# Half and whole slots share first products and transposes; VectorE adds the halves (two MoE layers behind a sparse attention)

## The chip, the cores and the metric

One Trainium2 chip, one of its cores. The metric is the device time of the program in microseconds; a run's time is that of one execution, and the profile is of one execution with its own time. PE is the engine of the matrix products (PEld its weight loads), DVE is VectorE, ACT is ScalarE, POOL is GpSimd, SP issues most transfers.

## What is computed

Attention over 2304 tokens of width 512 (local windows and global tokens), and then twice a layer of experts: every token picks one of 8 experts, and the layer is two products with that expert's weights.

```python
def _moe_ref(x, expert_emb, tau, w1, w2):
    ...
    expert_idx = np.argmax(logits, axis=1)
    ...
    for e in range(8):
        mask = expert_idx == e
        h = np.maximum(x[mask] @ w1[e], 0.0)      # 512 -> 1024
        out[mask] = gate_w[mask, None] * (h @ w2[e])   # 1024 -> 512
def reference(**kwargs):
    ...
    x = _moe_ref(x=x, **moe_kwargs)
    return _moe2_ref(x=x, **moe2_kwargs)   # the same, with a second gate
```

## The kernel before, in words

After the attention each layer sorts its tokens by expert into slots of 128 rows. There are 21 slots in the main path of a layer (three more are code that runs only with over 21 slots in use), and which expert a slot belongs to is known only when the kernel runs. So the code is one stretch per slot, written out for all slots, and branches inside it pick what a slot needs by a mode that PE, ACT and DVE read into registers (`look_mode`, L794; `flag`, L774):

- M_HALF (0): at most 64 tokens, which happens in the last slot of an expert;
- M_FOLLOW (1) and M_LEAD (3): two neighbouring slots of one expert that are multiplied together, all of it in the lead's stretch, while the follower runs two tiny placeholder products (`little`);
- M_SOLO (2): a whole slot by itself. Slot 0 of a layer has no mode and runs as a whole slot.

Products are made of float32 numbers split in two parts, high and low: high by high, high by low and low by high are summed in PSUM. A whole slot needs 24 products of 128x512 for the first layer of weights (`mm1`, L927), then 8 transposes of the result (`hsplit`, L991), ReLU and split into high (ACT) and low (DVE), and 24 products for the second (`mm2`, L1044). A half slot puts the high parts of its 64 tokens in columns 0 to 63 of one operand and their low parts in columns 64 to 127. Then 8 products with the high weights and 8 with the low weights (the latter with the 64 high columns alone, L940 with `m=HALF`) do, and `hsplit` adds the two halves while it turns them: 8 products of float32 by the matrix `twice`, 128x64, two identities over each other (L999). In `mm2` a half slot has 16 products (`half_products`, L986); what its rows 64 to 127 gathered is added on DVE (L1081).

The order of one step s on PE is: `mm1(s)`, in layer 0 the routing work of earlier slots (transposes L1098, products L233 and L240, L1167 and L1168), `mm2(s-1)` in two stretches of four weight blocks with the transposes of slot s+2 between them (L850, `xsplit`), `hsplit(s)`. In the same step ACT copies and DVE subtracts the next expert's weights into high and low parts (`split1`, `split2`, L757 to L767: 1024 columns per instruction), if the next slot belongs to another expert. The order is written by hand; the queues run in order on each engine, and semaphores join them.

`any_of` (L818) and `either` (L798) write the branches. Where one arm of a branch is empty, the engine that skips the other arm runs an instruction that waits for its own earlier work and then adds to its semaphore what the skipped arm would have added. Before the change both arms of PE's branches in the slots hold products.

Of the kernel before, what the change touches and what calls it, by code (L numbers as in the profile page):

```python
# [9 lines left out]
F32 = mybir.dt.float32  # L10
# [4 lines left out]
AF = mybir.ActivationFunctionType  # L15
ALU = mybir.AluOpType
AX = mybir.AxisListType
# [3 lines left out]
P = 128  # L21
# [10 lines left out]
HALF = P // 2  # L32
# [3 lines left out]
M_HALF, M_FOLLOW, M_SOLO, M_LEAD = range(4)  # L36
# [4 lines left out]
XR = 3  # L41
# [64 lines left out]
def sparse_attention_two_moe(ctx, tc, qt, kt, vx, vn, qg, emb, tau, w1a, w2a, wgo, w1b, w2b, cs1, cs2, out):  # L106
    nc = tc.nc
    V, S, G, T, SP = nc.vector, nc.scalar, nc.gpsimd, nc.tensor, nc.sync
# [25 lines left out]
    twice = cp.tile([P, HALF], F32, name="twice")  # L134
# [526 lines left out]
    class Slots:  # L661
# [265 lines left out]
        def mm1(self, s, amid=None):  # L927
            self.room(s)
            if self.leads(s):
                self.room(s + 1)  # L930
            ph = [ps_h.tile([P, 512], F32, name="ph") for n in range(2)]
            self.ph[s] = [ps_ht.tile([P, 512], F32, name="pht") for n in range(2)]
            self.h[s] = [mp.tile([P, 512], F32, name=f"hs{n}", bufs=1) for n in range(2)]
            ws = [[(w1h[k][:, n * 512:(n + 1) * 512], w1l[k][:, n * 512:(n + 1) * 512]) for n in range(2)]
                  for k in range(4)]

            def some(x, part, first, last, m=P):
                for k in range(4):
                    for n in range(2):
                        T.matmul(ph[n][:m], lhsT=x[:, k, s % XR, :m], rhs=ws[k][n][part], start=first and k == 0,  # L940
                                 stop=last and k == 3, skip_group_check=True)

            def half():

                some(xh, 0, True, False)
                some(xh, 1, False, True, HALF)

            def whole():
                some(xh, 0, True, False)
                some(xh, 1, False, False)  # L950
                some(xl, 0, False, True)

            def full(ks):
                for k in ks:
                    for n in range(2):
                        self.full_products(ph[n], xh[:, k, s % XR], xl[:, k, s % XR], *ws[k][n], k == 0, k == 3)

            def little():

                for p in ph:  # L960
                    T.matmul(p[:, 0:1], lhsT=onesb, rhs=ones[:, 0:1], start=True, stop=True)

            if amid:
                for a, z in zip([0] + sorted(amid), sorted(amid) + [4]):
                    if a:
                        amid[a]()
                    full(range(a, z))
            else:
                arms = {T: (half, little, whole, lambda: self.lead_products(s, ph, 0))}

            def keep():
                for n in range(2):
                    S.copy(self.h[s][n], ph[n])  # L973

            if amid:
                keep()
            else:
                self.any_of(s, {**arms, S: (keep, None, keep, None)})
            return ph

        def full_products(self, out, ah, al, bh, bl, first, last):
            T.matmul(out, lhsT=ah, rhs=bh, start=first, stop=False, skip_group_check=True)
            T.matmul(out, lhsT=ah, rhs=bl, start=False, stop=False, skip_group_check=True)
            T.matmul(out, lhsT=al, rhs=bh, start=False, stop=last, skip_group_check=True)

        def half_products(self, out, a, bh, bl, first, last):  # L986

            T.matmul(out, lhsT=a, rhs=bh, start=first, stop=last, skip_group_check=True)
            T.matmul(out[:HALF], lhsT=a[:, :HALF], rhs=bl, start=False, stop=last, skip_group_check=True)

        def hsplit(self, s, later=None):  # L991
            hs, pos = self.h.pop(s), self.ph.pop(s)
            pts = [p.rearrange("p (k t) -> p k t", k=4) for p in pos]
            his, los = self.room(s)

            def half():
                for pt, h in zip(pts, hs):
                    for k in range(4):
                        T.matmul(pt[:, k, :HALF], lhsT=h[:, k * P:(k + 1) * P], rhs=twice, start=True, stop=True)  # L999

            def full():
                for pt, h in zip(pts, hs):
                    for k in range(4):
                        T.transpose(pt[:, k, :], h[:, k * P:(k + 1) * P], ident)

            def half_low():
                for pt, hi in zip(pts, his):
                    V.scalar_tensor_tensor(out=hi[:, :, HALF:], in0=pt[:, :, :HALF], scalar=0.0,
                                           in1=hi[:, :, :HALF].bitcast(F32), op0=ALU.max, op1=ALU.subtract)

            def full_low():
                for pt, hi, lo in zip(pts, his, los):
                    V.scalar_tensor_tensor(out=lo, in0=pt, scalar=0.0, in1=hi.bitcast(F32),
                                           op0=ALU.max, op1=ALU.subtract)

            def little():
                for p in pos:
                    T.matmul(p[:, 0:1], lhsT=onesb, rhs=ones[:, 0:1], start=True, stop=True)

            single = [lambda: [S.activation(hi[:, :, :HALF], pt[:, :, :HALF], AF.Relu) for pt, hi in zip(pts, his)],  # L1020
                      lambda: [S.activation(hi, pt, AF.Relu) for pt, hi in zip(pts, his)]]
            arms = {T: (half, little, full, lambda: self.lead_products(s, pos, 1)), S: (single[0], None, single[1], None)}
            if later is None:
                arms[V] = (half_low, None, full_low, None)
            self.any_of(s, arms)
            if later is not None:
                later += [lambda pt=pt, hi=hi, lo=lo: V.scalar_tensor_tensor(
                    out=lo, in0=pt, scalar=0.0, in1=hi.bitcast(F32), op0=ALU.max, op1=ALU.subtract)
                    for pt, hi, lo in zip(pts, his, los)]
            return pos  # L1030
# [13 lines left out]
        def mm2(self, s, amid=None, after=None, last=False):  # L1044
            his, los = self.hT.pop(s)
            hT = [(hi[:, k, :], lo[:, k, :]) for hi, lo in zip(his, los) for k in range(4)]
            py = (ps_h.tile([P, DM], F32, name="pye", tag="ph") if s + self.l == 0 else
                  ps_ht.tile([P, DM], F32, name="pyl", tag="pht") if last else ps_y.tile([P, DM], F32, name="py"))
            amid = amid or {}

            def ws(k):
                return w2h[k // 2][:, k % 2], w2l[k // 2][:, k % 2], k == 0, k == 7

            def whole(ks):

                for x, w in ((0, w2h), (1, w2h), (0, w2l)):
                    for k in ks:
                        T.matmul(py, lhsT=hT[k][x], rhs=w[k // 2][:, k % 2], start=k == 0 and x == 0 and w is w2h,  # L1058
                                 stop=k == 7 and w is w2l, skip_group_check=True)

            if s + self.l == 0:
                self.mm2_early(py, hT)
            for a, z in zip([0] + sorted(amid), sorted(amid) + [8]) if s + self.l else ():
                if a:
                    amid[a]()
                self.either(s, {T: (lambda: [self.half_products(py, hT[k][0], *ws(k)) for k in range(a, z)],
                                    lambda: whole(range(a, z)))})
            if after:
                after()
            yr = (mp.tile([P, DM], F32, name="yr", bufs=3) if s or self.l else  # L1070
                  sm.tile([P, DM], F32, name="yr0", tag="sq1", bufs=1))
            gate = self.gt.pop(s)[:, 0:1]
            S.activation(yr, py, AF.Copy, scale=gate)  # L1073
            self.y[s] = yr

            if (s, V.engine) not in self.mode:
                return
            yl = mp.tile([P, DM], F32, name="yl", tag="yT")[:HALF]

            def half():  # L1080
                V.scalar_tensor_tensor(out=yr[:HALF], in0=yl, scalar=gate[:HALF], in1=yr[:HALF],  # L1081
                                       op0=ALU.mult, op1=ALU.add)

            self.either(s, {S: (lambda: S.copy(yl, py[HALF:]), None), V: (half, None)})
# [289 lines left out]
    first = First(0)  # L1374
# [13 lines left out]
    xh, xl = [wx.tile([P, 4, XR, P], F32R, name=f"x{w}") for w in "hl"]  # L1388
# [9 lines left out]
    for v in range(3):  # L1398
        m = c[:, C_MASK + v * P:C_MASK + (v + 1) * P].rearrange("p (a t) -> p a t", a=4)
# [406 lines left out]
    def rest():  # L1806
        yield from norms
        yield from r4.gating()
        yield from [None] * 4
        yield from r4.storing(S)  # L1810
        yield from r3.storing()
# [81 lines left out]
```

## Time and profile before

| what | us |
|---|---|
| runs of the kernel before | 733.7, 737.54, 743.43 (median 737.54) |
| the profiled execution, its own time | 737.24 |
| its span, first to last instruction | 735.5 |
| PE busy | 648.6 (88%) |
| DVE busy | 422.3 (57%) |
| ACT busy | 361.4 (49%) |

The attention takes the span to about 172 us, layer 0's slots run from there to about 470 us, layer 1's from about 480 us to the end. An execution's own time is 1.7 us more than its span. A view of lines groups instructions by source line; a timeline merges neighbours of one line and gives the idle time of the engine ahead of them in brackets, with what ended it. "issue" as the cause is an engine that waited for nothing that the profile shows; a name with q is the engine's sequencer, which runs branches and semaphore instructions.

### The profile page before, as it was taken

To read this page: it belongs to the slowest core of one execution; us is meant where nothing else is said; L and a number is where in the kernel's file an instruction comes from. 1 tells how busy PE (TensorE), PEld (TensorE's weight loads), DVE (VectorE), ACT (ScalarE), POOL (GpSimd) and SP (SyncE) were. 2 spreads that over 40 slices of the span, in tenths; PEclk is the share of its full clock that TensorE was granted. 3 is DMA by queue.
4 is the path that set the end of the run, shared out by engine and by line. 5 is a ranking of instruction groups with operands and counts; after the bars stand their busy time and mean duration, and the time that the engine had idled before them with its cause. 6 is when DMAs were issued, how large, how long until landed. Compare 5 with 4: busy or idle time off the path is not lost. (4 is left out here: it accounts for less than half of the span.)

```text
span 735.5 us, 20018 instructions
## 1 busy us (share of the span) xinstructions
PE 648.6 (88%) x6289; PEld 522.6 (71%) x6297; DVE 422.3 (57%) x1210; ACT 361.4 (49%) x881; POOL 214.9 (29%) x291
## 2 busy tenths in 40 slices
PE   7877776877999899898898989798999999999994
PEld 3555454556878798787676867577797889788893
DVE  4657878895226845467467877741474444364340
ACT  3667766821234633455355744411574444473540
POOL 3453636104412211131120500041243324245131
PEclk9999999988999899999999999899999999999998
DMA  9984949303437514548567425233756444736500
GB/s 277 265 288 143 304 118 259 86 23 75 143 108 217 161 46 143 173 137 234 165 168 211 124 90 204 85 91 133 271 184 243 150 163 156 239 107 205 179 27 27
DMA packets 55156, 118.05 MB, mean 161 GB/s; under 512 B 13800, under 2 KB 15336, under 8 KB 54961
## 3 DMA queue, kind: packets, MB, share of 16 engines
q1 hardware_dynamic: 44544, 87.21, 38.4%
q0 software_dynamic: 9344, 27.91, 12.3%
q8 instruction: 98, 1.61, 1.0%
q14 instruction: 98, 0.79, 0.5%
q10 hardware_dynamic: 1072, 0.53, 0.3%
HBM read 100.11 MB, written 16.30 MB: 158 GB/s over the span
## 5 line engine op out<-in xcount | busy, mean ns | idle before, releaser
L643 DVE TENSOR_TENSOR kq<-st,kq 128x1024 fp32r<-128x1024 f32 x64 | 75.4, 1220 | 70.7 <-ACT kq L765 62.8
L643 DVE TENSOR_TENSOR w2l<-st,w2h 128x1024 fp32r<-128x1024 f32 x64 | 74.4, 1219 | 13.1 <-ACT w2h L765 9.5
L1089 POOL DMA_INDIRECT out<-yr,ti x21 | 34.1, 1622 | 149.8 <-ACTq L757 71.3
L680 POOL DMA_INDIRECT xrow<-xs,idx x40 | 51.0, 1274 | 91.3 <-DVE all L592 37.7
L1058 PE MATMUL py<-w2h,hh 128*128 128x512 f32 x240 | 71.7, 421 | 3.2 <-issue 3.1
L940 PE MATMUL ph<-kq,xh 128*128 128x512 f32 (+1 forms) x256 | 64.4, 404 | 5.8 <-DVEq L757 1.3
L1058 PE MATMUL py<-w2l,hh 128*128 128x512 f32 x240 | 66.4, 399 | 0.7 <-issue 0.7
L1058 PE MATMUL py<-w2h,hl 128*128 128x512 f32 x240 | 66.4, 399 | 0.0
L1073 ACT ACTIVATE yr<-py,gt 128x512 f32<-128x512 f32 x39 | 26.8, 688 | 68.5 <-PE py L1058 43.6
L765 ACT CAST kq<-st 128x1024 fp32r<-128x1024 f32 x56 | 55.9, 1048 | 4.3 <-ACTq L740 2.8
L940 PEld LDWEIGHTS ph<-kq,xh 128*128 128x128 f32 (+1 forms) x256 | 43.5, 175 | 20.4 <-issue 2.8
L892 PE MATMUL ph<-xh,kq 128*128 128x256 f32 x384 | 53.8, 302 | 4.8 <-DVE xl L854 2.2
L765 ACT CAST w2h<-st 128x1024 fp32r<-128x1024 f32 x56 | 54.5, 1047 | 5.7 <-ACTq L827 3.4
L696 POOL TENSOR_SCALAR va<-gt 128x1 f32<-128x1 f32 x21 | 4.6, 220 | 174.6 <-DVE oh L1123 174.2
L892 PEld LDWEIGHTS ph<-xh,kq 128*128 128x128 f32 x384 | 51.3, 208 | 5.2 <-ACTq L757 1.6
L1058 PEld LDWEIGHTS py<-w2l,hh 128*128 128x128 f32 x240 | 46.2, 192 | 11.5 <-issue 1.1
L1058 PEld LDWEIGHTS py<-w2h,hl 128*128 128x128 f32 x240 | 46.2, 193 | 10.8
L892 PE MATMUL pht<-xh,kq 128*128 128x256 f32 x384 | 49.6, 285 | 4.1 <-ACTq L757 2.1
L680 POOL DMA_INDIRECT gt<-gs,idx x40 | 47.8, 1194 | 17.4 <-issue 8.6
L892 PEld LDWEIGHTS pht<-xh,kq 128*128 128x128 f32 x384 | 47.2, 191 | 7.0 <-ACTq L757 3.0
L1058 PEld LDWEIGHTS py<-w2h,hh 128*128 128x128 f32 x240 | 42.4, 194 | 9.8 <-issue 3.3
L973 ACT COPY hs<-ph 128x512 f32<-128x512 f32 x34 | 18.4, 589 | 61.5 <-PE ph L940 59.1
(540 smaller groups left out, 1348.4 us busy)
## 6 DMA issues: line engine op xcount, KB each, us to landing
st<-in_w1a SPq DMA_DIRECT2D x32, 512.0 KB, 6.8
st<-in_w2a SPq DMA_DIRECT2D x32, 512.0 KB, 5.1
st<-in_w1b SPq DMA_DIRECT2D x32, 512.0 KB, 6.7
st<-in_w2b SPq DMA_DIRECT2D x32, 512.0 KB, 7.0
xs<-yr SPq DMA_DIRECT2D x21, 256.0 KB, 7.7
kq<-in_kt POOLq DMA_DIRECT2D x3, 1728.0 KB, 9.3
xs<-xrow SPq DMA_DIRECT2D x17, 256.0 KB, 4.2
vw<-in_vx SPq DMA_DIRECT2D x26, 128.0 KB, 7.6
```

Of the source, the lines that this page charges most:

```text
L643: V.tensor_sub(lo[k], st[k], hi[k].bitcast(F32))
L680: G.indirect_dma_start(out=to, out_offset=None, in_=rows_[self.l][:n, :], in_offset=bass.IndirectOffsetOnAxis(ap=idx, axis=0), bounds_chec ...
L696: G.tensor_scalar(out=self.va[s], in0=tok, scalar1=FAR, scalar2=None, op0=ALU.is_lt)
L765: S.copy(hi[k], st[k])
L892: T.matmul(po, lhsT=w[k][:, f * P:(f + 1) * P], rhs=x[:, k, at], start=first and k == 0 and f % 2 == 0, stop=last and k == 3, skip_group_c ...
L940: T.matmul(ph[n][:m], lhsT=x[:, k, s % XR, :m], rhs=ws[k][n][part], start=first and k == 0, stop=last and k == 3, skip_group_check=True)
L973: S.copy(self.h[s][n], ph[n])
L1058: T.matmul(py, lhsT=hT[k][x], rhs=w[k // 2][:, k % 2], start=k == 0 and x == 0 and w is w2h, stop=k == 7 and w is w2l, skip_group_check=True)
L1073: S.activation(yr, py, AF.Copy, scale=gate)
L1089: G.indirect_dma_start(out=out, out_offset=bass.IndirectOffsetOnAxis(ap=self.ti.pop(s), axis=0), in_=yr, in_offset=None, bounds_check=NTOK ...
```

## The change

`half` and `whole` of `mm1`, of `hsplit` and of `mm2` become one stretch each that both run, and what only whole slots need stands behind a branch without an Else:

- `mm1`: the 8 products with the high weights and the 8 with the low weights, now all with 128 columns of the left operand, are shared (`shared`); the 8 with the low part of x (`rest`) stand behind `m > M_HALF`. The order of the tests is another: lead first, then follow, then the shared stretch.
- `hsplit`: half slots run the 8 transposes of whole slots. DVE then sums the two halves of a half slot out of PSUM into two new tiles `hsum`, in a branch of its own in front of the one for the split, and ACT and DVE read these tiles in place of PSUM.
- `mm2`: in each stretch high by high, then high by low run for all; low by high stands behind `m > M_HALF`. Half slots use all 128 columns for the low weights too.

```diff
+            def shared():
                 some(xh, 0, True, False)
-                some(xh, 1, False, True, HALF)
-            def whole():
-                some(xh, 0, True, False)
-                some(xh, 1, False, False)
+                some(xh, 1, False, True)
+            def rest():
                 some(xl, 0, False, True)
...
-                arms = {T: (half, little, whole, lambda: self.lead_products(s, ph, 0))}
+                self.first_products(s, shared, rest, little, lambda: self.lead_products(s, ph, 0))
...
+        def first_products(self, s, shared, rest, little, lead):
+            m = self.mode.get((s, T.engine))
+            if m is None:
+                shared()
+                if rest:
+                    rest()
+                return
+            def single():
+                with tc.If(m == M_FOLLOW) as follows:
+                    little()
+                with follows.Else():
+                    shared()
+                    if rest:
+                        with tc.If(m > M_HALF):
+                            rest()
+            if self.leads(s):
+                with tc.If(m > M_SOLO) as both:
+                    lead()
+                with both.Else():
+                    single()
+            else:
+                single()
...
-            def half():
-                for pt, h in zip(pts, hs):
-                    for k in range(4):
-                        T.matmul(pt[:, k, :HALF], lhsT=h[:, k * P:(k + 1) * P], rhs=twice, start=True, stop=True)
...
-            arms = {T: (half, little, full, lambda: self.lead_products(s, pos, 1)), S: (single[0], None, single[1], None)}
+            self.first_products(s, full, None, little, lambda: self.lead_products(s, pos, 1))
+            arms = {S: (single[0], None, single[1], None)}
+            if (s, V.engine) in self.mode:
+                sums = [mp.tile([P, 4, HALF], F32, name="hsum", bufs=2) for _ in pts]
+                with tc.If(self.mode[s, V.engine] < M_FOLLOW):
+                    for a, pt in zip(sums, pts):
+                        V.tensor_reduce(a, pt.rearrange("p k (h t) -> p k t h", h=2), axis=AX.X, op=ALU.add)
...
-                self.either(s, {T: (lambda: [self.half_products(py, hT[k][0], *ws(k)) for k in range(a, z)],
-                                    lambda: whole(range(a, z)))})
+                some(0, w2h, range(a, z), True)
+                some(0, w2l, range(a, z))
+                self.either(s, {T: (None, lambda: some(1, w2h, range(a, z)))})
```

## Rows read from the trace of the kernel before

**Rows 1.** Busy time by stretch: layer 0's slots, then layer 1's.

```profile
172.00:470.00 298.00, 273.74 (x1761) 225.39 (x1760) 175.81 (x521) 141.39 (x274) 62.67 (x102) 0.97 0.52 151
...
480.00:735.50 255.50, 237.55 (x1404) 200.98 (x1402) 108.55 (x177) 112.41 (x182) 83.93 (x81) 0.99 0.47 157
```

**Rows 2.** Waits of PE after 172 us: total, times, longest.

```profile
PE pr L1167 <- DVE oh L1123: 6.1, 4, 3.8
PE py L1058 <- issue: 3.7, 2, 3.1
PE pp L233 <- DVE lg L1116: 3.5, 3, 1.4
PE ptm L850 <- issue: 2.4, 1, 2.4
PE ph L892 <- DVE xl L854: 2.2, 3, 1.3
```

**Rows 3.** Groups by line and shape on PE and its weight loads.

```profile
L940 PE MATMUL ph<-kq,xh 128*64 128x512 f32 x80 | 20.7, 401 | 0.0
L999 PE MATMUL pht<-twice,hs 128*128 128x64 f32 x160 | 19.3, 274 | 0.1
...
L940 PEld LDWEIGHTS ph<-kq,xh 128*128 128x128 f32 x176 | 32.4, 191 | 12.8 <-issue 2.2 <-ACTq L757 1.4 <-ACTq L811 1.2
...
L940 PEld LDWEIGHTS ph<-kq,xh 128*64 128x64 f32 x80 | 11.1, 139 | 7.6 <-issue 0.6 <-DVE hh L1008 0.2
```

**Rows 4.** Timeline of PE at a half slot of layer 1 (start, length).

```profile
569.59 1.89 PE L999 MATMUL pht<-twice,hs 128*128 128x64 f32 x16
571.29 4.08 PE L892 MATMUL ph<-xh,kq 128*128 128x256 f32 x32
...
577.36 0.39 PE L989 MATMUL py<-w2l,hh 128*64 128x512 f32 x1
577.59 0.40 PE L988 MATMUL py<-w2h,hh 128*128 128x512 f32 x1
577.82 0.39 PE L989 MATMUL py<-w2l,hh 128*64 128x512 f32 x1
```

**Rows 5.** Timeline of PE at a whole slot of layer 1.

```profile
687.12 1.04 PE L1004 MATMUL pht<-c,hs 128*128 128x128 f32 x8
687.91 3.93 PE L940 MATMUL ph<-kq,xh 128*128 128x512 f32 x16
```

**Rows 6.** Sequencer of PE by line: ns min/median/max.

```profile
L1835 PEldq EVENT_SEMAPHORE  x1: 51/51/51, 727.2 to 727.2; - x1
...
L825 PEldq COMPARE_BRANCH  x80: 70/218/2212, 175.4 to 714.5; - x80
...
L827 PEldq COMPARE_BRANCH  x72: 65/176/2268, 175.6 to 712.5; - x72
```

**Rows 7.** Groups by line and shape on DVE and ACT.

```profile
L1509 DVE TENSOR_REDUCE amx<-s__231 128x4 f32<-128x512 f32 x1 | 0.7, 692 | 2.9 <-PE s__232 L1498 2.9
L1008 DVE SCALAR_TENSOR_TENSOR hh<-pht,hh 128x256 fp32r<-128x256 f32 x20 | 7.5, 419 | 2.3 <-ACT hh L1020 2.2
L1020 ACT ACTIVATE hh<-pht 128x256 fp32r<-128x256 f32 x20 | 6.7, 384 | 8.3 <-PE pht L999 7.0 <-ACT yl L1084 0.9 <-DVE kq L643 0.4
```

**Rows 8.** Timeline of DVE: one skipped arm, then a half slot of layer 1.

```profile
227.83 0.29 DVE L235 COPY sp<-pp 128x128 f32<-128x128 f32 x1 [0.15 <-DVEq L811]
...
571.80 0.76 DVE L1008 SCALAR_TENSOR_TENSOR hh<-pht,hh 128x256 fp32r<-128x256 f32 x2 [0.43 <-ACT hh L1020]
577.95 1.42 DVE L908 SCALAR_TENSOR_TENSOR hl<-ph,hh 128x256 fp32r<-128x256 f32 x4 [5.39 <-ACT hh L906]
```

**Rows 9.** Timelines of DVE and ACT at a half slot of layer 0.

```profile
416.11 0.74 DVE L1008 SCALAR_TENSOR_TENSOR hh<-pht,hh 128x256 fp32r<-128x256 f32 x2
...
425.04 1.42 DVE L908 SCALAR_TENSOR_TENSOR hl<-ph,hh 128x256 fp32r<-128x256 f32 x4 [1.71 <-ACT yr L1073]
...
413.09 0.70 ACT L1020 ACTIVATE hh<-pht 128x256 fp32r<-128x256 f32 x2 [0.87 <-ACT yl L1084]
```

More of the change, by code (lines that the diff above doesn't have):

```diff
@@ L935, in mm1, with some @@
                   for k in range(4)]
-            def some(x, part, first, last, m=P):
+            def some(x, part, first, last):
                 for k in range(4):
                     for n in range(2):
-                        T.matmul(ph[n][:m], lhsT=x[:, k, s % XR, :m], rhs=ws[k][n][part], start=first and k == 0,
+                        T.matmul(ph[n], lhsT=x[:, k, s % XR], rhs=ws[k][n][part], start=first and k == 0,
                                  stop=last and k == 3, skip_group_check=True)
-            def half():
+            def shared():
                 some(xh, 0, True, False)
-                some(xh, 1, False, True, HALF)
-            def whole():
-                some(xh, 0, True, False)
-                some(xh, 1, False, False)
+                some(xh, 1, False, True)
+            def rest():
                 some(xl, 0, False, True)
@@ L977, in mm1 @@
             else:
-                self.any_of(s, {**arms, S: (keep, None, keep, None)})
+                self.any_of(s, {S: (keep, None, keep, None)})
             return ph
+        def first_products(self, s, shared, rest, little, lead):
[20 more added lines that the diff above has]
+                single()
         def full_products(self, out, ah, al, bh, bl, first, last):
@@ L984, in full_products @@
             T.matmul(out, lhsT=al, rhs=bh, start=False, stop=last, skip_group_check=True)
-        def half_products(self, out, a, bh, bl, first, last):
-            T.matmul(out, lhsT=a, rhs=bh, start=first, stop=last, skip_group_check=True)
-            T.matmul(out[:HALF], lhsT=a[:, :HALF], rhs=bl, start=False, stop=last, skip_group_check=True)
         def hsplit(self, s, later=None):
@@ L994, in hsplit @@
             his, los = self.room(s)
-            def half():
-                for pt, h in zip(pts, hs):
-                    for k in range(4):
-                        T.matmul(pt[:, k, :HALF], lhsT=h[:, k * P:(k + 1) * P], rhs=twice, start=True, stop=True)
             def full():
@@ L1006, in half_low @@
             def half_low():
-                for pt, hi in zip(pts, his):
-                    V.scalar_tensor_tensor(out=hi[:, :, HALF:], in0=pt[:, :, :HALF], scalar=0.0,
-                                           in1=hi[:, :, :HALF].bitcast(F32), op0=ALU.max, op1=ALU.subtract)
+                for a, hi in zip(sums, his):
+                    V.scalar_tensor_tensor(out=hi[:, :, HALF:], in0=a, scalar=0.0, in1=hi[:, :, :HALF].bitcast(F32),
+                                           op0=ALU.max, op1=ALU.subtract)
             def full_low():
@@ L1018, in little @@
                     T.matmul(p[:, 0:1], lhsT=onesb, rhs=ones[:, 0:1], start=True, stop=True)
-            single = [lambda: [S.activation(hi[:, :, :HALF], pt[:, :, :HALF], AF.Relu) for pt, hi in zip(pts, his)],
+            single = [lambda: [S.activation(hi[:, :, :HALF], a, AF.Relu) for a, hi in zip(sums, his)],
                       lambda: [S.activation(hi, pt, AF.Relu) for pt, hi in zip(pts, his)]]
-            arms = {T: (half, little, full, lambda: self.lead_products(s, pos, 1)), S: (single[0], None, single[1], None)}
+            self.first_products(s, full, None, little, lambda: self.lead_products(s, pos, 1))
[5 more added lines that the diff above has]
+                        V.tensor_reduce(a, pt.rearrange("p k (h t) -> p k t h", h=2), axis=AX.X, op=ALU.add)
             if later is None:
@@ L1049, in mm2, with some @@
             amid = amid or {}
[L1051 to L1059, printed above, removed]
+            def some(x, w, ks, first=False):
+                for k in ks:
+                    T.matmul(py, lhsT=hT[k][x], rhs=w[k // 2][:, k % 2], start=first and k == 0, stop=k == 7,
+                             skip_group_check=True)
             if s + self.l == 0:
```

## The prediction

> **What bounds the kernel now.** I read the busy time by stretch first, and there only from 172 us on, because the change touches nothing of the attention. PE is busy 273.7 of 298.0 us in layer 0's slots and 237.6 of 255.5 us in layer 1's; DVE and ACT are near a half [rows 1]. So PE's stream sets the time, above all in layer 1, and a microsecond taken from or put into that stream counts nearly whole. The second view is PE's waits [rows 2]: the large ones are short and few. Three of the five are for DVE (6.1, 3.5 and 2.2 us), all in places where DVE has the routing or the weight split in its queue; the other two are "issue" (3.7 and 2.4 us), PE's own sequencer being late after a branch. Third, how many slots of which kind there are, which no line of code tells: the 64-column products are 80, 8 to a slot, so ten slots are half [rows 3], of the 40 that have a mode; the other 30 are lead, follow or solo. In the timeline five of the ten lie in layer 0 and five in layer 1. What follows is ten times the balance of one half slot, and a small term for the other thirty.
>
> **Transposes of half slots.** Before: 16 instructions (each product of float32 by `twice` runs as two, 160 for ten slots [rows 3]), from 569.59 to 571.29, when the next work starts: 1.70 us [rows 4]. After: the 8 transposes that whole slots have, 687.12 to 687.91: 0.79 us [rows 5]. Removed: 0.91 us per half slot, 9.1 us for ten.
>
> **Wider products.** The number of products in `mm1` and `mm2` of a half slot stays 16 each, and none gets more columns of the moving operand. What grows is the weight load, 139 to 191 ns on average [rows 3]. In the timeline a 64-column product is followed after 0.23 us, and a 128-column one after 0.23 us as well [rows 4]: the load hides under the product before it, as long as there is one. Cost 0. The Trainium skill, TensorE: Matmul & The Clock Gate, section "LDWEIGHTS (loading the stationary operand)", has the load's time grow with the columns, which the 139 and 191 ns bear out; if the loads stood in line, 16 of them would cost 16 x 0.052 = 0.83 us per half slot, and the sum below would be 8.3 us higher. The equal steps of 0.23 us speak against that.
>
> **The empty arms on PE.** This is the term that I weigh most. `rest` in `mm1` and the low-by-high stretch in `mm2` now stand behind branches with no other arm. A half slot skips one in `mm1` and one in each stretch of `mm2`: three, and two more in the last slot of layer 0, whose `mm2` has four stretches: 32 in all. An engine that skips waits for its own earlier work and then raises its semaphore. PE does that once in the whole trace of before, after the last slot, where an EVENT_SEMAPHORE of 51 ns stands at L1835 [rows 6]; nothing follows there whose delay could be read. DVE does it often, and one skip leaves it idle for 0.15 us [rows 8]. For PE I work it out: products overlap, each lasts 0.39 us and the next starts after 0.23 [rows 4], so waiting for the last one's end loses 0.16; the next weight load, 0.19 [rows 3], is no longer under a product; the semaphore instruction is 0.05. Sum 0.40 us per skip. Bounds: 0, if the sequencer's own run-ahead already ends at such places, and 0.80, if the branch that comes next is laid bare each time too and costs its median of 0.18 to 0.22 us [rows 6] and as much again to get going. I take 0.40, since each of its parts is a row. Behind a waiting PE stands everything that it has still to do: the transposes of later slots, and through them ACT's copies. The third skip of a half slot stands just ahead of the branches of `hsplit`, of which I add 0.15 us as laid bare. One half slot then pays 3 x 0.40 + 0.15 = 1.35 us and gets 0.91 back: +0.44.
>
> **DVE's sum.** Two reductions of 128x512 into 128x256 from PSUM. The nearest row is a reduction of the same 512 elements from PSUM, 692 ns [rows 7]; bounds 0.42 (the split of 256 elements [rows 7]) and 1.0 (if the stride of the halves costs half as much again). With 0.69 each, DVE gets 1.4 us per half slot, and ACT's ReLU (384 ns each [rows 7]), which waited for PE, now waits for DVE. In layer 1 this is covered: after its half-slot work DVE waits 5.39 us for ACT, and that for PE's next products [rows 8]; the slot's result is wanted only after the next slot's `mm1`. The weight split that the next `mm1` needs stands ahead of the sum in DVE's queue. In the crowded end of layer 0, where short experts follow each other, the cover is thin: at 416.11 DVE comes to the half slot well after ACT, which had done its ReLU at 413.09 and gone on to the weights; after that DVE has 1.71 us of slack left [rows 9]. There ACT would stand at the ReLU until DVE has summed, with 4 us of weight copies queued behind it. I count three half slots of this kind (two in the crowd, and the last slot of the layer, whose result is wanted at once), 1.3 us each, +4, and no gain from PE's shorter stream there, as DVE is last; without any cover, all ten would cost 14.
>
> **The other thirty slots.** DVE skips one more arm in each, 0.15 us [rows 8]; ACT only tests the mode. On the path only where PE then waits for DVE, of which PE's waits have some dozen [rows 2]: 12 x 0.15 = +1.8, cut to +1, as in some of them DVE stands at the weights first. In `mm2` the low part is wanted later and w2's low part earlier than before; no wait of PE for either is among the large ones [rows 2], so 0. PE's code becomes shorter, the arms that are jumped over too. The two "issue" waits of 6.1 us together [rows 2] may change either way; some branches took 2.2 us against a median of 0.2 [rows 6]. I take -1.5.
>
> **Sum.** Seven half slots in which PE is last, 7 x 0.44 = +3.1; three in which DVE is, +4; the others +1; code -1.5: +6.6 us. Against the profiled execution's 737.24 us this is 743.8, and since the median of the runs is 737.54, it stands for the median too: 744 us, 0.9% slower. A change of 2%, 14.7 us, is about what a measurement of this kernel can tell from none, as its three runs lie 9.7 us apart.
>
> **Rivals.**
> - The skips cost nothing, and the transposes are a plain gain. For: PE already runs 152 tests at two lines alone [rows 6], and of the large waits only two are "issue" [rows 2]. Against: those tests wait for nothing, while the skip waits for the end of the products, however early it was read. Time: 10 x -0.91, of which the three slots led by DVE keep nothing, -6.4, and -1.5 of code, +2 of DVE: 731 us, with 726 to 737 for the bounds of DVE's sum.
> - The skip lays bare what comes after it. At the end of a half slot's `mm2` PE's sequencer has to fetch the code of `hsplit`; if a jump there takes the 2.2 us of the longest branches [rows 6] in most of the ten slots, +15 to 20 us on top of the 3 x 0.40 less 0.91. It decides from about six of ten on: 755 to 765 us, slower by over 2%. Against: the median branch is 0.2 us, and the shared stretches have shorter jumps.
> - Shorter code is the main effect. PE has few but long branches, up to 2.27 us at L827 [rows 6], and 6.1 us of "issue" stand in its largest waits [rows 2]; take those away, the whole 9.1 us of transposes, and no cost of a skip: 722 us. The Trainium skill, Runtime: NRT & Kernel Launch, section "Instruction fetch mechanics", says that a taken branch out of the pages at hand stalls until its page is fetched; the few branches of over 2 us look like that. It is unlikely to take all of it, as the jump over the lead's products stays.
>
> **How the numbers follow.** Forecast as above 0.58, with 737 to 752 from the bounds of the skip (0.15 to 0.65 us would be -6 to +6 of its 9); skips free 0.28; skips that lay bare fetches 0.08; shorter code 0.04; the rest, 0.02, elsewhere. For 8 in 10 the range takes in most of the first rival: 728 to 752. Faster by over 2% (below 722.8) 0.04; slower by over 2% (above 752.3) 0.07; within 2% 0.89.
>
> **What would show it.** In the changed profile: 80 more transposes at `hsplit`'s line and none of the 160 products by `twice`; PE's EVENT_SEMAPHOREs at `either`'s and `first_products`' branches, some 32, each with an idle PE of about 0.4 us behind it, by "issue" or by PE itself; on DVE 20 reductions of about 0.7 us; ACT's half-slot ReLU waiting for DVE. If PE's idle time behind the skips sums to under 5 us, the forecast falls to the first rival; if DVE's reductions take over 1 us, or PE waits for DVE in layer 1 after half slots, it is higher.

## The result, and the profile after

The changed kernel takes 741.88 us (median, 738.79 to 751.38) against 737.83 for the kernel before on the same chip (731.42 to 743.43), 20 runs each: ratio 1.0065, 95% interval 1.0042 to 1.0088, so 4.8 us slower, 3.1 to 6.5. The ratio is taken over the runs in the fast state alone, so it is a little above the quotient of the two medians. The profiled execution took 740.11 us, its span is 738.3.

Busy time by stretch, the layers' slots, of the changed kernel (columns as in [rows 1]):

```profile
172.00:470.00 298.00, 267.53 (x1691) 222.15 (x1689) 180.11 (x539) 135.14 (x262) 60.67 (x106) 0.97 0.51 151
480.00:738.30 258.30, 239.13 (x1408) 202.29 (x1408) 123.86 (x228) 114.73 (x187) 77.94 (x81) 0.98 0.45 154
```

In the same 298 us of layer 0 PE is busy 6.2 us less than in [rows 1]. Some 4.5 of that is the transposes' shorter work in five half slots (0.9 us each, below), so the figure alone does not tell how much more PE waits. PE's waits after 172 us (total, times, longest):

```profile
PE pr L1183 <- DVE oh L1139: 9.6, 5, 3.8
PE pl L240 <- DVE sp L235: 2.4, 1, 2.4
PE ptm L850 <- PEq L805: 2.2, 7, 0.4
PE py L1073 <- PEq L994: 1.5, 5, 0.3
PE pht L892 <- PEq L805: 1.3, 3, 0.4
PE ph L940 <- issue: 1.0, 1, 1.0
PE pty L1114 <- PEq L994: 0.6, 2, 0.3
```

Three things differ from [rows 2]. The waits for PE's own sequencer (PEq) at L805 and L994 are the skips, 5.6 us in these rows. The waits for DVE grew: `oh` from 6.1 to 9.6, and `sp` with 2.4 is new. And the two "issue" waits of 3.7 and 2.4 us are gone; the largest is 1.0. PE's sequencer by line (ns min/median/max), first one line of the kernel before and then the changed kernel:

```profile
L805 PEldq COMPARE_BRANCH  x140: 72/176/5299, 192.5 to 722.2; - x140
```

```profile
L805 PEldq EVENT_SEMAPHORE  x22: 51/51/51, 236.7 to 711.4; - x22
L994 PEldq EVENT_SEMAPHORE  x10: 51/51/51, 219.9 to 694.2; - x10
L998 PEldq COMPARE_BRANCH  x100: 70/216/1701, 178.5 to 715.5; - x100
```

The queue of instruction packets, before and after:

```profile
q8 instruction: 98, 1.61, 1.0%
```

```profile
q8 instruction: 83, 1.36, 0.8%
```

At the lines of the branches there are 22 + 10 = 32 EVENT_SEMAPHOREs, the skips, where [rows 6] had one. (Others stand at lines of products, in the kernel before too, and are not counted.) The longest branch inside the slots is 1.70 us; before, L805 had one of 5.30 us. The instruction packets are 83 instead of 98. Groups by line and shape, which answer to [rows 3] and [rows 7]:

```profile
L1018 PE MATMUL pht<-c,hs 128*128 128x128 f32 x144 | 20.1, 283 | 2.7 <-ACT kq L765 2.0 <-issue 0.6
L940 PEld LDWEIGHTS ph<-kq,xh 128*128 128x128 f32 x256 | 49.0, 197 | 13.8 <-ACT zs L1155 2.2 <-issue 1.4 <-ACT ex L1154 0.2
```

```profile
L1042 DVE TENSOR_REDUCE hsum<-pht 128x256 f32<-128x512 f32 x20 | 12.8, 682 | 1.5 <-DVEq L811 1.5
L1022 DVE SCALAR_TENSOR_TENSOR hh<-hsum,hh 128x256 fp32r<-128x256 f32 x20 | 8.5, 425 | 1.2 <-ACTq L757 0.2
L1034 ACT ACTIVATE hh<-hsum 128x256 fp32r<-128x256 f32 x20 | 8.3, 418 | 30.8 <-DVE hsum L1042 29.7
```

All products load 128 columns, the 160 products by `twice` are gone, a sum takes 0.68 us, and ACT's ReLU waits 29.7 us in all for it. PE's timeline at a half slot of layer 1, which answers to [rows 4]:

```profile
573.19 1.03 PE L1018 MATMUL pht<-c,hs 128*128 128x128 f32 x8
573.99 4.07 PE L892 MATMUL ph<-xh,kq 128*128 128x256 f32 x32
...
580.75 1.07 PE L1073 MATMUL py<-w2l,hh 128*128 128x512 f32 x4
582.12 0.63 PE L850 MATMUL ptm<-c,xrow 128*128 128x128 f32 x4 [0.30 <-PEq L805]
582.50 1.18 PE L1073 MATMUL py<-w2h,hh 128*128 128x512 f32 x4
583.51 1.08 PE L1073 MATMUL py<-w2l,hh 128*128 128x512 f32 x4
585.02 4.06 PE L892 MATMUL pht<-xh,kq 128*128 128x256 f32 x32 [0.43 <-PEq L805]
```

Transposes: 573.19 to 573.99, 0.80 us instead of 1.70. A skip is read from two groups: the product before it ends at 583.51 + 1.08 = 584.59, and the next starts at 585.02, 0.43 later. Where nothing is skipped, the next starts before the last has ended: 583.51 against 582.50 + 1.18 = 583.68, 0.17 earlier. This skip costs 0.43 + 0.17 = 0.60 us, the two others of a half slot 0.30 + 0.17 = 0.47 each: 1.54 in all, against 0.90 from the transposes.

DVE at the same half slot, which answers to [rows 8]:

```profile
575.04 1.29 DVE L1042 TENSOR_REDUCE hsum<-pht 128x256 f32<-128x512 f32 x2 [0.30 <-DVEq L811]
...
580.64 1.42 DVE L908 SCALAR_TENSOR_TENSOR hl<-ph,hh 128x256 fp32r<-128x256 f32 x4 [3.41 <-ACT hh L906]
```

After the sum and its low part DVE still waits 3.41 us for ACT: here the sum is covered.

The end of layer 0, DVE and then PE:

```profile
453.78 4.63 DVE L643 TENSOR_TENSOR kq<-st,kq 128x1024 fp32r<-128x1024 f32 x4
458.33 1.28 DVE L1042 TENSOR_REDUCE hsum<-pht 128x256 f32<-128x512 f32 x2
...
461.64 0.29 DVE L235 COPY sp<-pp 128x128 f32<-128x128 f32 x1 [1.07 <-DVEq L811]
```

```profile
458.53 0.43 PE L233 MATMUL pp<-yT,wg 128*32 128x128 f32 x8
...
461.99 0.40 PE L240 MATMUL pl<-d,sp 128*128 128x16 f32 x2 [2.40 <-DVE sp L235]
462.23 1.07 PE L1073 MATMUL pyl<-w2h,hh 128*128 128x512 f32 x2
```

In the last slot DVE comes to the sum only after a weight split of 4.63 us, so ACT's ReLU, DVE's low part and the copy `sp` that the routing waits for are all later. PE has computed `pp` at 458.5, runs out of other work 2.40 us ahead of 461.99, and stands until then.

### The profile page after: what moved, and what is told of

Its sections match the earlier page's. It is cut to its first block, busy times and chain, and to the rows that moved or that the text cites. A ratio compares the mean times of both kernels' runs of the same rounds, so it can differ in the third digit from the quotient of the medians.

```text
span 738.3 us, 20062 instructions
## 1 busy us (share of the span) xinstructions
PE 648.4 (88%) x6217; PEld 523.3 (71%) x6217; DVE 433.9 (59%) x1230; ACT 363.1 (49%) x881; POOL 202.9 (27%) x291
## 3 DMA queue, kind: packets, MB, share of 16 engines
q0 software_dynamic: 9344, 27.91, 12.1%
## 5 line engine op out<-in xcount | busy, mean ns | idle before, releaser
L1073 PE MATMUL py<-w2h,hh 128*128 128x512 f32 x312 | 91.4, 415 | 1.6 <-PEq L994 1.5
L1073 PE MATMUL py<-w2l,hh 128*128 128x512 f32 x312 | 85.1, 395 | 0.0
L643 DVE TENSOR_TENSOR w2l<-st,w2h 128x1024 fp32r<-128x1024 f32 x64 | 74.4, 1219 | 14.5 <-ACT w2h L765 10.1
L1073 PEld LDWEIGHTS py<-w2l,hh 128*128 128x128 f32 x312 | 59.1, 190 | 13.7
L940 PE MATMUL ph<-kq,xh 128*128 128x512 f32 x256 | 65.4, 410 | 3.5 <-ACT zs L1155 2.1
L1105 POOL DMA_INDIRECT out<-yr,ti x21 | 24.6, 1170 | 150.4 <-ACT w2h L765 24.5
L1073 PE MATMUL py<-w2h,hl 128*128 128x512 f32 x240 | 64.9, 392 | 0.0
L1073 PEld LDWEIGHTS py<-w2h,hh 128*128 128x128 f32 x312 | 53.4, 190 | 11.3 <-issue 3.5
L940 PEld LDWEIGHTS ph<-kq,xh 128*128 128x128 f32 x256 | 49.0, 197 | 13.8 <-ACT zs L1155 2.2
L696 POOL TENSOR_SCALAR va<-gt 128x1 f32<-128x1 f32 x21 | 4.6, 220 | 177.7 <-DVE oh L1139 177.3
L680 POOL DMA_INDIRECT gt<-gs,idx x40 | 45.8, 1146 | 18.5 <-issue 11.0
```

The source lines that it names most:

```text
L643: V.tensor_sub(lo[k], st[k], hi[k].bitcast(F32))
L680: G.indirect_dma_start(out=to, out_offset=None, in_=rows_[self.l][:n, :], in_offset=bass.IndirectOffsetOnAxis(ap=idx, axis=0), bounds_chec ...
L696: G.tensor_scalar(out=self.va[s], in0=tok, scalar1=FAR, scalar2=None, op0=ALU.is_lt)
L940: T.matmul(ph[n], lhsT=x[:, k, s % XR], rhs=ws[k][n][part], start=first and k == 0, stop=last and k == 3, skip_group_check=True)
L1073: T.matmul(py, lhsT=hT[k][x], rhs=w[k // 2][:, k % 2], start=first and k == 0, stop=k == 7, skip_group_check=True)
L1105: G.indirect_dma_start(out=out, out_offset=bass.IndirectOffsetOnAxis(ap=self.ti.pop(s), axis=0), in_=yr, in_offset=None, bounds_check=NTOK ...
```

## The experiments

Each kernel ran beside the kernel before: E1 to E4 on one chip, E5 to E8 on a second, E9 to E12 on a third. The kernel before took 741.61, 739.67 and 742.69 us there (medians), so kernels are compared by their ratios to it and not by their times. For reading the profiles, the span is cut at the starts of the leads' first products in PE's timeline (us; no lead follows the last one of layer 0 until layer 1 begins):

| kernel | attention | layer 0 to its last lead | last lead to layer 1 | layer 1 | ratio, 95% |
|---|---|---|---|---|---|
| before | 176.8 | 236.4 | 73.8 | 248.5 | 1 |
| changed | 179.2 | 235.9 | 80.7 | 242.5 | 1.0065 (1.004 to 1.009) |
| E1 | 177.9 | 236.5 | 79.5 | 235.2 | 0.9902 (0.987 to 0.993) |
| E2 | 180.1 | 239.1 | 75.3 | 252.0 | 1.0079 (1.004 to 1.012) |
| E3 | 178.2 | 234.6 | 81.1 | 237.9 | 0.9945 (0.991 to 0.998) |
| E4 | 179.0 | 240.2 | 80.4 | 248.4 | 1.015 (1.009 to 1.021) |
| E5 | 178.9 | 233.0 | 74.4 | 246.1 | 0.989 (0.984 to 0.994) |
| E6 | 184.6 | 236.2 | 76.4 | 236.2 | 0.9896 (0.984 to 0.995) |
| E7 | 183.4 | 235.6 | 76.6 | 242.2 | 0.9988 (0.996 to 1.002) |
| E8 | 180.7 | 232.7 | 74.7 | 236.3 | 0.976 (0.970 to 0.982) |
| E9 | 178.7 | 233.3 | 74.9 | 234.8 | 0.9757 (0.971 to 0.980) |
| E10 | 181.1 | 235.1 | 75.2 | 237.3 | 0.9804 (0.976 to 0.985) |
| E11 | 177.7 | 234.0 | 73.6 | 236.6 | 0.9774 (0.974 to 0.981) |
| E12 | 178.3 | 233.6 | 75.2 | 236.6 | 0.9841 (0.979 to 0.989) |

E8 and E12 are one program twice, and E10 and E11 turned out to hold its work too (below). So equal work differs by up to 1.0 us in layer 1, 1.6 at the end of layer 0, 2.4 in the column before, 3.4 in the attention, and 0.008 in the ratio; smaller differences say nothing.

**E1, no empty arms.**

```
-            some(xh, 1, False, True)                # in shared()
+            some(xh, 1, False, True, slice(0, 7))
-                with tc.If(m > M_HALF):
-                    rest()
+                with tc.If(m > M_HALF) as which:
+                    end(); rest()                   # end(): the eighth product
+                with which.Else():
+                    end()
```

and the same with each stretch's last low product in `mm2`.

> The changed kernel, but no branch of TensorE in mm1 and mm2 has an empty arm any more: the last shared product (one of 16 in mm1, one of each stretch's low products in mm2) stands in both arms instead of ahead of the branch. The same products run, DVE's sum stays. Theory (each of the 32 skips costs TensorE about 0.45 us, 0.69 from product to product instead of 0.23): some 13 to 14 us less than the changed kernel, about 728 us, ratio 0.986 to the kernel before. Rival A (the cost lies in DVE's sum and in routing at the end of layer 0, the skips are free): about 741, ratio 1.005. Rival B (the gain in layer 1 came from shorter code; the duplicated product changes the code little): as the theory, so this run does not tell B apart.

Measured: 735.24 us, 0.9902, which is 0.0163 or 12.1 us below the changed kernel: 0.38 us for each of 32 skips. At the lines of its branches no EVENT_SEMAPHORE of PE is left. PE at the place of the second and third skip:

```profile
577.67 0.60 PE L850 MATMUL ptm<-c,xrow 128*128 128x128 f32 x4
578.02 1.17 PE L1079 MATMUL py<-w2h,hh 128*128 128x512 f32 x4
579.03 1.09 PE L1079 MATMUL py<-w2l,hh 128*128 128x512 f32 x4
579.96 3.99 PE L892 MATMUL pht<-xh,kq 128*128 128x256 f32 x32
```

The branches are still there, yet PE has no gap. It is the empty arm that costs. Layer 1 is 7.3 us shorter for its 15 skips, 0.49 each; the end of layer 0 stays at 79.5, so the skips are not what lengthened it. Rival A falls.

**E2, products only,** with `hsplit` put back as it was before.

> mm1 and mm2 of the changed kernel (shared stretches, empty arms), hsplit as before (16 products by two stacked identities for a half slot, no sum on DVE). Theory (skips 0.45 us each, 22 of the 32 stand in mm1 and mm2 when hsplit keeps its four arms, at least those with a next product: +10 to +14; code shorter, -4 to -6 in layer 1): about 744 to 748 us, ratio 1.008 to 1.014. Rival A (skips free, DVE's sum is the cost): 732 to 737 us, ratio 0.993 to 0.999.

Measured: 748.53 us, 1.0079; all 32 skips are in it. The end of layer 0 is back at 75.3, so most of what it grew by, 6.9 us in the changed kernel, comes with the new `hsplit`.

**E3, the turn only,** that is the new `hsplit` with `mm1` and `mm2` as before.

> mm1 and mm2 as before (an arm for each kind of slot, no empty arm), hsplit of the changed kernel (8 transposes for every slot, DVE sums the halves). Theory (transposes -0.9 us in each of ten half slots = -9; DVE's sum lays some 4 to 7 us bare at the end of layer 0; nothing for skips): 732 to 736 us, ratio 0.992 to 0.997. Rival A (DVE's sum is what made the changed kernel slower): 741 us or more, ratio 1.004 or more.

Measured: 737.65 us, 0.9945, 4.1 us faster, as the theory had it, but as a difference of two larger numbers: the end of layer 0 is 7.3 us longer and layer 1 is 10.6 shorter. Of the 10.6, 5.9 lie between layer 1's first two leads, where the kernel before has the branch of 5.30 us; the remaining 4.7 lie in the stretches of the four other half slots. What that branch costs in the kernel before:

```profile
506.00 1.02 PE L850 MATMUL ptm<-c,xrow 128*128 128x128 f32 x4 [2.39 <-issue]
506.66 2.06 PE L1058 MATMUL py<-w2h,hh 128*128 128x512 f32 x4
```

PE stands 2.39 us, and the four products behind it then take 2.06 us where E3's take 1.17. E3 has no such wait there, though only `hsplit` was changed: part of E3's gain is that a long branch is gone, and not the transposes.

**E4, more skips.**

```
+                c = (a + z) // 2
+                self.either(s, {T: (None, lambda: some(1, w2h, range(a, c)))})
                 some(0, w2l, range(a, z))
-                self.either(s, {T: (None, lambda: some(1, w2h, range(a, z)))})
+                self.either(s, {T: (None, lambda: some(1, w2h, range(c, z)))})
```

> The changed kernel with the low-by-high stretch of mm2 cut in two, one half ahead of the shared low products and one behind, each behind a branch with an empty arm: a half slot skips one more time in each stretch, 22 skips more on TensorE, all products the same. Theory (0.45 us each): 22 x 0.45 = +9.9 over the changed kernel, about 751 us, ratio 1.019, and 54 of TensorE's own semaphore instructions. Rival A (skips are free): the changed kernel's time, 742 us, ratio 1.006.

Measured: 754.17 us, 1.015; 0.0085 or 6.3 us over the changed kernel for 22 more skips, 0.29 each (its interval allows 0.1 to 0.5). The sequencer's rows count them:

```profile
L805 PEldq EVENT_SEMAPHORE  x44: 51/51/51, 235.2 to 721.0; - x44
```

In layer 1 of its profile ten more skips cost 5.9 us, 0.59 each. The edit also moves half of a whole slot's low-by-high products ahead; what that does by itself was not measured here.

**E5, both arms, products by `twice`:** E1's `mm1` and `mm2` with E2's `hsplit`.

> The kernel before in all work and all operations of every slot (16 products by two stacked identities, no sum on DVE), with only the form of mm1's and mm2's code changed: shared stretches, the last shared product in both arms, so no empty arm on TensorE; a half slot's low products load 128 columns of weights instead of 64. Theory (the shorter code of mm1 and mm2 is worth 3 to 7 us by itself, wider weight loads nothing): ratio 0.991 to 0.996 to the kernel before. Rival (code length is worth nothing; the gain of layer 1 in the changed kernel was transposes alone): 0.999 to 1.001. Rival 2 (the wider weight loads cost 0.05 us each, 160 of them): 1.005 or more.

Measured: 733.12 us, 0.989, 8.1 us faster (4.4 to 11.8) with the same operations on every engine but for the wider loads and the order of `mm2`'s products. So the form of the code is worth something by itself, about as much as was expected or more, and the rival of wider loads that cost 0.05 us each falls. E2 differs from E5 by the 32 skips and the form of their branches alone: 0.0189, 14 us, 0.44 each. The waits for the sequencer in E5 after 172 us:

```profile
PE py L1078 <- issue: 1.6, 1, 1.6
PE pht L1043 <- issue: 0.4, 1, 0.4
```

That is 2.0 us where [rows 2] has 6.1 in its two largest. The other 4 of the 8 us are not found in one place.

**E6 and E7, the last slot of layer 0 with the old `hsplit`,** on E1 and on the changed kernel.

```
-    self.mm2(s - 1, {4: lambda: self.hsplit(s)}, ...)
+    self.mm2(s - 1, {4: lambda: self.hsplit_by_products(s) if then else self.hsplit(s)}, ...)
```

> E1 (no empty arm on TensorE), and in the last slot of layer 0 alone hsplit as before (16 products, no sum on DVE). Theory (DVE's sum in that one slot, queued behind a weight split of 4.63 us and ahead of the copy sp that the routing waits for, costs some 6 us; the other nine sums nothing): E1's ratio 0.990 less 0.008, so 0.982, and the stretch from the last lead of layer 0 to the first of layer 1 back from 79.5 to some 74 us. Rival (the end of layer 0 is longer for another reason, such as the moved products or the gathers): 0.990 and 79 us again.

> The changed kernel with that one edit alone: hsplit as before in the last slot of layer 0. Theory: the changed kernel's ratio 1.0065 less 0.007 to 0.008, so 0.998 to 1.000; the skips stay. Rival (the end of layer 0 is longer for another reason): 1.006.

Measured: E7 0.9988, which is 0.0077 or 5.7 us below the changed kernel, as the theory said. E6 0.9896, no less than E1: a miss. In both profiles the end of layer 0 is shorter (3.1 us in E6, 4.1 in E7), but not back to 74. E6's profiled execution spent 6.7 us more in the attention, whose code is untouched; with an interval of 0.011 and repeats that differ by 0.008, E6 alone decides nothing. DVE and PE in E7 at that place:

```profile
461.14 0.75 DVE L1069 SCALAR_TENSOR_TENSOR hh<-pht,hh 128x256 fp32r<-128x256 f32 x2
462.94 0.29 DVE L235 COPY sp<-pp 128x128 f32<-128x128 f32 x1 [1.05 <-DVEq L811]
```

```profile
462.24 0.43 PE L233 MATMUL pp<-yT,wg 128*32 128x128 f32 x8
...
463.28 0.40 PE L240 MATMUL pl<-d,sp 128*128 128x16 f32 x2
463.53 0.70 PE L1114 MATMUL pyl<-w2h,hh 128*128 128x512 f32 x2
```

From `pp` to `pl` it is 1.04 us, where the changed kernel took 3.46.

**E8, the old `hsplit` in all of layer 0,** on E1 (`if self.l == 0: return self.hsplit_by_products(s, later)`).

> E1 with hsplit as before in every slot of layer 0 and the transposes with DVE's sum in layer 1 alone. Theory (only the last slot's sum costs; the other four half slots of layer 0 lose 0.9 us each of the transposes' gain as far as TensorE is the last there): 0.982 to 0.987, not below E6. Rival, as the prediction had it (three half slots of layer 0 are led by DVE and each pays about 1.3 us): 2 to 3 us less than E6, about 0.979.

Measured: 724.71 us, 0.976, and in the same program as E12 0.9841; both lie below E1. So it isn't the last slot alone. In the table its end of layer 0 is 74.7 (75.2 in E12) against 76.4 and 76.6 with the last slot alone undone, a difference not much over that between repeats. Between the two leads before, which hold two half slots, the stretch is 83.1 to 85.5 us in the four programs with E8's work, against 88.6 in E1 and 88.0 in E6. That is the rival's reading: several half slots of layer 0 pay for the sum.

**E9, the old order of `mm2`'s stretches,** on E8: the arm with the low-by-high products ahead of the shared low ones.

> E8 with mm2's stretches in the old order: high by high (its last product in both arms of the branch), then, in the arm of a whole slot, low by high, then high by low. Code length and products as in E8. Theory (the gain of shared code is its length, not the new order of the stretches): E8's ratio, 0.976, within 0.004 either way. Rival (the gain comes from w2's low part being taken before the slot's own low part, which DVE makes last): 3 us or more above E8, 0.980 to 0.985.

Measured: 724.45 us, 0.9757. That lies within the repeats of E8 (0.976 to 0.984), so no worth of the new order is seen, either way.

**E10 and E11, an arm that is never taken, of one and of 48 products,** on E8 (`with tc.If(m > 99) as no: never()`).

> E8 with one more branch on TensorE in each single slot's mm1, ahead of the test for a follower; its arm holds one product and is never taken. It is the control for the next kernel. Both theories: E8's time plus at most one short branch of 0.15 us in each of the slots where TensorE's sequencer is late, 0.976 to 0.982.

> As the control with the short arm, but the arm that is never taken holds 48 products (what sharing took out of a slot's code, roughly): the same instructions run, only more code has to be jumped over. Theory (the length of TensorE's code costs time by stalls of the sequencer after jumps): 4 to 8 us above the control, ratio higher by 0.005 to 0.011, more idle time of TensorE that is put down to issue, and more instruction-queue packets, 95 or more against 86. Rival (length is free; what the sharing saved is the tests and waits of the arms themselves): the control's ratio within 0.003.

Measured: 728.12 us, 0.9804, and 724.93 us, 0.9774. The pair says nothing of code length: in E8, E10 and E11 alike PE runs 353 branches and the queue has 86 instruction packets, so the added test and its arm are not in the programs (the mode can't be above 99). They count as repeats of E8. Whether it is the length of the code that costs stays open.

**E12, E8 again.**

> E8 once more, beside the three kernels made from it, and as the version that is to beat both kernels: ratio 0.970 to 0.982 again, layer 0 from its first lead to layer 1's first lead in 307 to 309 us as in E8, and the attention, whose code is the same in all kernels, anywhere between 177 and 185 us.

Measured: 728.24 us, 0.9841 (0.979 to 0.989), a little outside the range expected; layer 0 took 308.8 us and the attention 178.3, as expected. Over the four programs with E8's work the ratio is 0.976 to 0.984: this version is some 2% faster than the kernel before and 2.7% faster than the changed one.

## Why the prediction was right, and where its terms were not

The forecast was 744 us, the measurement 741.88, and the main mechanism held. Two terms were mis-sized in opposite directions, so the sum is closer than its parts: that it came within 2 us is in part luck. Measured terms are ratios times 740 us:

| term on the path | predicted | measured |
|---|---|---|
| skips on PE | 7 x 1.35 = +9.5 | +12.1 (E1 from the changed kernel), +14 (E2 from E5) |
| transposes and DVE's sum together | -6.4 + 4 = -2.4 | -4.1 (E3), -1.0 (changed kernel from E2), +0.9 (E1 from E5) |
| form of PE's code | -1.5 | -8.1 (E5), -3.2 (E1 from E3) |
| other thirty slots | +1 | not measured by itself |
| all | +6.6 | +4.8 |

The measured terms depend on what they are added to: one way from the kernel before to the changed one is E3, E1, changed (-4.1 - 3.2 + 12.1), another is E5, E2, changed (-8.1 + 14.0 - 1.0). E3's -4.1 holds the lost branch of 5.30 us, which is a matter of the code's form; the two other pairs for the transposes and the sum are near nothing, each with an interval of some 3 to 5 us either way.

- **Transposes, 0.91 us per half slot.** Right: 0.80 us instead of 1.70.
- **Wider products, 0.** Right: the four low products at 580.75 load 128 columns and take 1.07 us, which is 0.39 and three steps of 0.23, the step of [rows 4]; and E5, where all products load 128 columns, is not slower than the kernel before. The Trainium skill, TensorE: Matmul & The Clock Gate, section "LDWEIGHTS (loading the stationary operand)", has the load grow with its columns. The rows agree: 139 ns for 64 columns in [rows 3], 191 to 197 for twice as many. But a load that lies under a product lengthens nothing here, so the 8.3 us that would have followed if loads stood in line are not there.
- **Empty arms, 0.40 us each.** Right in kind, number (32) and nearly in size: 0.47 and 0.60 read from the timeline, 0.38, 0.44 and 0.29 from three timed pairs. The parts: the wait for the last product's end was 0.17 (0.16 forecast), the restart that nothing covers 0.30 to 0.43 (0.24 forecast). The idle time behind skips, 5.6 us in the rows above, is little over the 5 us at which the prediction would have gone over to free skips; but idle time leaves out the lost overlap of 0.17 us, and the timed cost is twice as much. The rival of free skips fell with E1, E2 and E4, that of bare fetches with the largest gap behind a skip in the changed kernel, 0.43 us.
- **Layer 0's skips.** The prediction counts 32 skips but prices 7 x 3 = 21; it left out those of three half slots led by DVE, and by its own 21 the bounds of the skip would be 5 us to either side and not 6. Whether they are free is not shown. In the profiles layer 0 as a whole is only 0.6 us shorter in E1, without its 17 skips, against 7.3 us for 15 in layer 1. But a lead of E1 ran there at a lower clock (below), and the timed difference of 12.1 us is 4.2 more than the two profiles show behind the attention. E2's layer 0 is 7.0 us longer than E5's, with a branch of 5.30 us and a single wait of 4.2 us for DVE in it.
- **DVE's sum.** Length right (0.68 against 0.69), cover in layer 1 right: after the sum and the low part DVE still waits 3.41 us for ACT. The mis-sized term is the price of a half slot led by DVE, 1.3 us, no more than the length of the sum itself. The last slot alone is 5.7 by E7 (4.1 in its profile), all of layer 0 some 8 (E8 and its repeats from E1, 4.5 to 10.5 by single runs), where the prediction has +4 for it. The sum's own 1.28 us is followed by ACT's ReLU and DVE's low part, which both start only when it has ended, and the routing's copy stands behind them in DVE's queue; the prediction names the weight split ahead of the sum, 4.63 us here, but gives the delay behind it no price.
- **Code.** The other mis-sized term is the -1.5. The prediction took 2.27 us for the longest branch and overlooked L805's 5.30. In the trace of the kernel before PE has nine branches of over 1 us inside the slots, 20.4 us together, though it does not stand for all of that; the changed kernel has one, of 1.70. The "issue" waits of 6.1 us went, as the prediction thought possible, and E5 shows a gain of 4.4 to 11.8 us with the same work. The Trainium skill, Runtime: NRT & Kernel Launch, section "Instruction fetch mechanics", has a taken branch that leaves the pages at hand stall for a fetch. The fall from 98 instruction packets to 83 and the loss of the 5.30 us branch agree with it, but no run here shows that a long branch is such a fetch. E2, with 88 packets, has a branch of 5.30 us too, at another line, and E5, with 89, still has five of over 1 us. Length, number of arms and where the pages fall were not told apart.

## What to carry to other kernels

An arm left empty is not free on an engine that sets the time: its skip waits until the engine's own work has ended, here 0.3 to 0.6 us each. Putting the last shared operation into both arms keeps the shared code and takes the wait away (E1: 12 us for 32 skips). Work that is moved to an engine with idle time should be placed slot by slot: look at what is queued ahead of it and behind it there; the same sum was covered in layer 1 and cost some 8 us in layer 0.

## What had not been expected of the hardware

PE's wait of 2.40 us at the end of layer 0 was followed by a lower clock, which the terms had no place for. Granted clock (the third column from the end) in the changed kernel and in E7, behind `pl`:

```profile
462.00:466.00 4.00, 3.85 (x13) 2.83 (x14) 3.11 (x17) 0.87 (x5) 0.00 (x0) 0.57 0.92 278
```

```profile
463.50:468.00 4.50, 3.99 (x28) 2.65 (x27) 3.61 (x20) 1.88 (x8) 0.00 (x0) 1.00 0.69 249
```

At 0.57 of 2.4 GHz, most of the stretch is at the lower level of 1.2, and a pair of products takes 1.07 us instead of 0.70. E1 has the same in another place, where PE was busy only 0.56 of the 2 us from 410 to 412 and waited again before a lead:

```profile
414.39 6.58 PE L892 MATMUL ph<-xh,kq 128*128 128x256 f32 x32 [0.55 <-DVE xl L854]
```

The clock there, in the same column as above:

```profile
416.00:420.00 4.00, 4.00 (x21) 4.00 (x20) 3.36 (x7) 1.82 (x4) 2.29 (x5) 0.50 0.03 1
```

The same lead takes 5.37 us in the changed kernel, also at a lower clock, and 4.07 in E8. So 1.3 to 2.5 us by which these two profiles are longer in layer 0 than E8's are clock. Not every wait is followed by a lower clock. The same wait of 2.10 us in the changed kernel and then in E7:

```profile
445.40 0.17 PE L1183 MATMUL pr<-oh,trib 128*128 128x8 bf16 x1 [2.10 <-DVE oh L1139]
...
445.78 5.27 PE L940 MATMUL ph<-kq,xh 128*128 128x512 f32 x16 [0.19 <-PE pr L1184]
```

```profile
449.56 0.17 PE L1224 MATMUL pr<-oh,trib 128*128 128x8 bf16 x1 [2.10 <-DVE oh L1180]
...
449.95 3.91 PE L940 MATMUL ph<-kq,xh 128*128 128x512 f32 x16 [0.19 <-PE pr L1225]
```

The 16 products behind it take 5.27 us in the one (granted clock 0.54) and 3.91 in the other (1.00). A wait on PE can thus cost more than its length, and a profile shows it only where it happened.

The attention took 176.8 to 184.6 us in these profiles with the same code in all kernels. With one profile for each kernel, a difference of a few us must be read from the stages that the change touches.
